# Turning the VectorE and ScalarE streams of a decode-attention kernel into hardware loops

## Chip, cores, metric

One core of one Trainium2 chip. The metric is device microseconds of one execution, as a median over runs; lower is better.

## The reference, cut to what matters

One token passes a block of attention over a long cache, beside a small feed-forward branch. With 32 heads of width 128 and 32768 cached positions in bf16, each head's K and each head's V are 8.39 MB. Together they are 537 MB of the 554 MB that the core reads.

```python
q = (xn @ wq).reshape(32, 128)                  # one token
scores = einsum("hd,hkd->hk", q, k) * 128**-0.5 # k: 32 x 32768 x 128
p = softmax(scores, -1)
o = einsum("hk,hkd->hd", p, v)
out = x + o.reshape(4096) @ wo + ffn(xn)
```

## The kernel before

SBUF holds a ring of three slots of 8.39 MB. SyncE streams wq, the feed-forward weights, K and V of every head and wo through it, and waits before each load until the slot's last reader has finished:

```python
for h in range(H):
    units.append(("k", h))
    if h >= 1: units.append(("v", h - 1))
units += [("wo",), ("v", H - 1)]
# SyncE, for each unit u in slot s
if s in owner: e.wait_ge(*owner.pop(s))
if u[0] == "k":
    e.dma_start(ring[:, s, :], kv_src(A_k_cache, u[1], 0, NJ)).then_inc(s_slot[s], 16)
    owner[s] = (s_qk, NHF * (u[1] + 1))     # free after TensorE has read the products
elif u[0] == "v":                           # the last V comes in five chunks (TAIL)
    e.dma_start(ring[:, s, :], kv_src(A_v_cache, u[1], 0, NJ)).then_inc(s_slot[s], 16)
    owner[s] = (s_pv, u[1] + 1)
```

For each head VectorE multiplies K by q in place, TensorE sums the products in part (against an identity), VectorE finishes the sums and the maximum, ScalarE takes the exponential, and TensorE multiplies by V one head later. TensorE's stream is already a hardware loop over groups of three heads. VectorE's and ScalarE's are written out for 32 heads:

```python
for h in range(H):                                    # VectorE
    v.wait_ge(s_qc, min(NQB, (h * DH) // 512 + 1))
    v.wait_ge(s_slot[s], 16 * use_of[u])              # K has landed
    q = qb[:, h * DH:(h + 1) * DH]
    for i in range(NHF):                              # 4 multiplies, 128 x 8192 bf16
        v.tensor_tensor(out=kh, in0=kh, in1=q[:, None, :].to_broadcast([128, HF, DH]),
                        op=ALU.mult).then_inc(s_mul, 1)
    ...                                               # 4 reduces, rz(h - 1)
    v.tensor_reduce(out=pmax[...], ...); v.wait_ge(s_t, h + 1)
    v.tensor_reduce(out=m1[...], ...);   v.wait_ge(s_b, h + 1)
    if h >= SR: v.wait_ge(s_exp, h - SR + 1)
    v.tensor_scalar(out=negb[...], ...).then_inc(s_neg, 1)

for h in range(H):                                    # ScalarE
    if h >= 3: column(h - 3)
    if h >= 2: evac(h - 2)
    a.wait_ge(s_neg, h + 1)
    ...                                               # two more waits
    a.activation(out=P[:, h % PR, :], in_=sc[:, :], func=ACTF.Exp, ...)
```

At the end TensorE has a long written-out tail: 155 products with wo for the first 31 heads, then 256 products with the last V, each a weight load and a product of one column:

```python
for h in range(H - 1): att(h)               # 5 products each
total(H - 1)
for i, n in enumerate(TAIL):                # pv_last: 256 products
    t.wait_ge(s_tail[i], 16)
    for _ in range(n):
        mm = t.matmul(OL, lhsT=ring[:, s, j*DH:(j+1)*DH], rhs=P[:, h % PR, j:j+1], ...)
        j += 1
```

## Time and profile before

| quantity | before |
|---|---|
| time, median of 3 runs | 1294.44 us (1294.24 to 1294.62) |
| bytes moved | 554.20 MB |
| share of DMA engines busy, middle of the run | 1.00 |
| VectorE idle before a head's first multiply | 2.8 us |
| instruction packets on queue 14 | 6 |

The first fence is the page of the profile. It gives each engine's busy time, the DMA totals, the queues (packets, MB, share of 16 engines' span), and the chain of work that ended last. PE is TensorE, PEld its weight loads, DVE VectorE, ACT ScalarE, POOL GpSimd, SPq SyncE's sequencer; L479 is line 479 of the kernel. The trace marks packets of the kind "instruction": six of 8192 bytes on queue 14 and nine on queue 8. They are taken for pieces of the engines' own programs, fetched while the program runs (in an experiment below, 1536 more VectorE instructions brought twelve more packets); below such a packet is called a refill.

```profile
span 1292.7 us, 9645 instructions
...
PE 1040.2 (80%) x5147; PEld 264.2 (20%) x3227; DVE 669.9 (52%) x407; ACT 50.8 (4%) x139; POOL 1.1 (0%) x8
...
DMA packets 14721, 554.20 MB, mean 429 GB/s; under 512 B 1329, under 2 KB 5490, under 8 KB 5746
...
q8 instruction: 9, 0.15, 0.0%
q14 instruction: 6, 0.05, 0.0%
...
DMA 54%; PE 30%; DVE 13%; issue 2%; SPq 1%; DVEq 0%
```

Next is the table by windows. Each row is a stretch of about three heads, with the busy time of the engines; the last three columns are the granted TensorE clock, the DMA share and GB/s.

```profile
core 0: us, PE busy (x) PEld busy (x) DVE busy (x) ACT busy (x) POOL busy (x), PEclk, DMA share, GB/s
366.60:482.80 116.20, 95.16 (x427) 22.43 (x246) 62.44 (x36) 4.11 (x12) 0.00 (x0) 0.90 1.00 433
715.00:831.00 116.00, 94.20 (x422) 22.03 (x241) 62.44 (x36) 4.10 (x12) 0.00 (x0) 0.90 1.00 433
```

In these stretches the DMA engines are busy all the time (share 1.00), at 433 GB/s. The chain of waits gives them only 54%, because it hops between loads and compute around the ring. The timeline of VectorE shows the slack (start, duration, what, then in brackets the idle time before and its releaser):

```profile
729.50 17.43 DVE L479 TENSOR_TENSOR ring<-ring,qb 128x8192 bf16<-128x8192 bf16 x4 [2.77 <-DMA ring<-in_A_k_cache_dram]
...
765.19 0.16 DVE L499 TENSOR_SCALAR negb<-ps 128x1 f32<-128x1 f32 x1 [6.94 <-PE ps L309]
769.18 4.43 DVE L479 TENSOR_TENSOR ring<-ring,qb 128x8192 bf16<-128x8192 bf16 x1 [3.83 <-DMA ring<-in_A_k_cache_dram]
```

VectorE is done with a head and then waits for the next K. The usual wait is 2.8 us. The last lines of the before kernel that matter are TensorE's in the tail:

```profile
1280.02 1.76 PE L279 MATMUL ps<-P,ring 128*128 128x1 bf16 x61
1282.06 3.55 PE L279 MATMUL ps<-P,ring 128*128 128x1 bf16 x128 [0.27 <-issue]
1285.80 1.50 PE L279 MATMUL ps<-P,ring 128*128 128x1 bf16 x51 [0.19 <-issue]
1287.88 0.59 PE L279 MATMUL ps<-P,ring 128*128 128x1 bf16 x16 [0.59 <-DMA ring<-in_A_v_cache_dram]
```

Its last 16 products wait for the last chunk of V: the end is bound by a landing.

### The profile page before, as it was taken

Reading aid. Unit: us, or ns where it says so; the run is one execution under the profiler, and the core shown is the slowest. Engines: PE = TensorE matmul, PEld = TensorE weight load, DVE = VectorE, ACT = ScalarE, POOL = GpSimd, SP = SyncE. Lnnn points to the kernel's source line nnn. Section 1 sums busy time; section 2 is a strip of 40 time slices with the busy share of each in tenths; the row PEclk is TensorE's granted clock in tenths of the full one; section 3 lists DMA queues with packets and bytes.
Section 4 is the critical chain, followed back from the end, with each engine's and each line's share of the span. In section 5 each row is a group of like instructions: output and inputs, shape, how many; then the busy total and the mean of one; then the engine's idle time right before and its main releaser. Section 6 shows DMA issues by size and latency. Waiting matters only on the chain.

```text
span 1292.7 us, 9645 instructions
## 1 busy us (share of the span) xinstructions
PE 1040.2 (80%) x5147; PEld 264.2 (20%) x3227; DVE 669.9 (52%) x407; ACT 50.8 (4%) x139; POOL 1.1 (0%) x8
## 2 busy tenths in 40 slices
PE   4688879877779877779877779877778877779878
PEld 1301222111222111222111222111222111222116
DVE  0485544666444666444666444666444666444660
ACT  2000000000000000000000000000000000000000
POOL 0000000000000000000000000000000000000000
PEclk9588899888899888889888889888899888899887
DMA  9999999999999999999999999999999999999997
GB/s 400 449 424 427 443 426 437 432 436 434 432 434 436 426 436 436 430 432 438 432 436 430 436 434 430 434 436 428 434 438 432 430 438 436 432 430 436 436 392 311
DMA packets 14721, 554.20 MB, mean 429 GB/s; under 512 B 1329, under 2 KB 5490, under 8 KB 5746
## 3 DMA queue, kind: packets, MB, share of 16 engines
q1 hardware_dynamic: 14704, 554.00, 99.4%
q8 instruction: 9, 0.15, 0.0%
q14 instruction: 6, 0.05, 0.0%
q10 hardware_dynamic: 2, 0.00, 0.0%
HBM read 553.99 MB, written 0.00 MB: 429 GB/s over the span
## 4 chain that ended last, share of the span: by engine, by line
DMA 54%; PE 30%; DVE 13%; issue 2%; SPq 1%; DVEq 0%
DMA ring<-in_A_k_cache_dram 52%; PE ps L266 16%; DVE ring L479 13%; PE ps L227 12%; DMA ring<-in_A_v_cache_dram 2%; PE ps L254 1%; SPq L174 1%; PE ps L303 0%; PE ps L297 0%; SPq L183 0%; DVE sc L485 0%; PE ps L279 0%; SPq L185 0%; DVE pmax L491 0%; SPq L182 0%
## 5 line engine op out<-in xcount | busy, mean ns | idle before, releaser
L479 DVE TENSOR_TENSOR ring<-ring,qb 128x8192 bf16<-128x8192 bf16 x128 | 557.8, 4421 | 88.4 <-DMA ring<-in_A_k_cache_dram 88.4
L227 PE MATMUL ps<-ring,ident 128*128 128x512 bf16 x1920 | 498.7, 418 | 0.0
L266 PE MATMUL ps<-ring,P 128*4 128x512 bf16 x1984 | 438.3, 379 | 0.0
L254 PE MATMUL ps<-ring,ident 128*128 128x512 bf16 x128 | 56.1, 439 | 224.2 <-DVE ring L479 223.6
L266 PEld LDWEIGHTS ps<-ring,P 128*4 128x4 bf16 x1984 | 166.0, 85 | 245.4
L254 PEld LDWEIGHTS ps<-ring,ident 128*128 128x128 bf16 x128 | 12.6, 99 | 622.2 <-DVE ring L479 350.4
L499 DVE TENSOR_SCALAR negb<-ps 128x1 f32<-128x1 f32 x32 | 5.1, 158 | 215.5 <-PE ps L309 215.5
L485 DVE TENSOR_REDUCE sc<-ps 128x64 f32<-128x512 f32 x128 | 82.3, 686 | 63.0 <-PE ps L227 63.0
L494 DVE TENSOR_REDUCE m<-ps 1x1 f32<-1x128 f32 x32 | 8.9, 278 | 192.2 <-PE ps L303 192.2
L403 ACT ACTIVATE P<-sc,negb 128x256 bf16<-128x256 f32 x32 | 16.2, 508 | 1185.1 <-DVE negb L499 1185.1
L297 PEld LDWEIGHTS ps<-rsum,ones 128*128 128x128 f32 x64 | 12.3, 194 | 99.1 <-issue 98.3
L289 PE MATMUL ps<-identf,o 4*128 4x1 f32 x248 | 31.8, 245 | 0.9 <-ACT o L386 0.9
L289 PEld LDWEIGHTS ps<-identf,o 4*128 4x128 f32 x248 | 30.0, 187 | 0.9 <-ACT o L386 0.9
L386 ACT ACTIVATE o<-ps,rzb 4x512 f32<-4x512 f32 x31 | 21.0, 677 | 0.0
L219 PE MATMUL ps<-ring 128*128 128x512 bf16 x40 | 11.3, 455 | 11.0 <-DMA ring<-in_A_wq_dram 11.0
L449 DVE TENSOR_SCALAR sg<-sg 128x13 f32<-128x13 f32 (+1 forms) x2 | 0.2, 156 | 34.2 <-ACT sg L379 34.2
L491 DVE TENSOR_REDUCE pmax<-sc 128x1 f32<-128x256 f32 x32 | 13.4, 420 | 0.0
L303 PE MATMUL ps<-identf,pmax 128*1 128x128 f32 x64 | 12.2, 273 | 1.2 <-DVE pmax L491 1.2
L330 PE MATMUL ps<-xn,ring 128*128 128x1 bf16 (+1 forms) x140 | 8.8, 199 | 4.6 <-DMA ring<-in_B_w_down_dram 4.6
L309 PE MATMUL ps<-m,ones 1*128 1x1 f32 x64 | 12.1, 256 | 0.4 <-DVE m L494 0.4
L309 PEld LDWEIGHTS ps<-m,ones 1*128 1x128 f32 x64 | 9.4, 182 | 14.2 <-issue 13.5
L468 DVE RECIPROCAL rzb<-ps 128x1 f32<-128x1 f32 x32 | 5.1, 158 | 9.8 <-PE ps L297 9.8
(50 smaller groups left out, 88.8 us busy)
## 6 DMA issues: line engine op xcount, KB each, us to landing
ring<-in_A_wq_dram SPq DMA_DIRECT2D x1, 5120.0 KB, 15.2
ring<-in_A_wo_dram SPq DMA_DIRECT2D x1, 5120.0 KB, 37.0
ring<-in_A_v_cache_dram SPq DMA_DIRECT2D x1, 4096.0 KB, 22.3
ring<-in_B_w_gate_dram SPq DMA_DIRECT2D x1, 2160.0 KB, 19.9
ring<-in_B_w_up_dram SPq DMA_DIRECT2D x1, 2160.0 KB, 24.6
ring<-in_B_w_down_dram SPq DMA_DIRECT2D x1, 2080.0 KB, 28.5
ring<-in_A_v_cache_dram SPq DMA_DIRECT2D x1, 2048.0 KB, 21.6
ring<-in_A_v_cache_dram SPq DMA_DIRECT2D x1, 1024.0 KB, 23.6
```

The lines of the kernel that those rows point to most:

```text
L174: e.dma_start(ring[:, s, j * DH:(j + n) * DH], kv_src(A_v_cache, u[1], j, n)).then_inc(s_tail[i], 16)
L227: return t.add_instruction(mybir.InstMatmult(start_tensor_calc=False, stop_tensor_calc=stop, tile_size=(128, 128), tile_position=(0, 0), l ...
L254: t.matmul(ob, lhsT=ident[:, :], rhs=src, start=True, stop=False)
L266: mm = t.matmul(O, lhsT=P[:, h % PR, j:j + W], rhs=ring[:, s, j * DH:(j + W) * DH], start=(j == 0), stop=(j + W == NJ))
L289: mm = t.matmul(fold_ps, lhsT=o4[:, m * DH:(m + 1) * DH], rhs=identf[0:W, m:m + 1], start=(m == 0), stop=(m == W - 1))
L297: t.matmul(misc[:, 129:130], lhsT=ones[:, :], rhs=rsum[:, h % SR:h % SR + 1], start=True, stop=True).then_inc(s_z, 1)
L309: t.matmul(misc[:, 128:129], lhsT=ones[0:1, :], rhs=m1[0:1, h % SR:h % SR + 1], start=True, stop=True).then_inc(s_b, 1)
L386: a.activation(out=o4[:, :], in_=O, func=ACTF.Copy, scale=rzb[0:W, h % SR:h % SR + 1]).then_inc(s_o4, 1)
L403: a.activation(out=P[:, h % PR, :], in_=sc[:, :], func=ACTF.Exp, bias=negb[:, h % SR:h % SR + 1], scale=c_scale, accum_out=rsum[:, h % SR: ...
L479: v.tensor_tensor(out=kh, in0=kh, in1=q[:, None, :].to_broadcast([128, HF, DH]), op=ALU.mult).then_inc(s_mul, 1)
L485: v.tensor_reduce(out=sc[:, i * HF:(i + 1) * HF], in_=bank[i].rearrange("p (j e) -> p j e", e=G), axis=AX.X, op=ALU.add).then_inc(s_red, 1)
L491: v.tensor_reduce(out=pmax[:, h % SR:h % SR + 1], in_=sc[:, :], axis=AX.X, op=ALU.max).then_inc(s_max, 1)
```

## The change

The intent is to give the two engines short programs: their streams become hardware loops of three heads a turn. Wait counts become register values (`group * d + n`), and the q and ocol addresses become register offsets. To make all counts positive and linear, ScalarE raises `s_ov` once at the start and its readers wait for one more. Waits that others imply are dropped. VectorE's loop starts at head 2, ScalarE's at head 5. The diff, cut:

```diff
+        def counter(e, h0):
+            group = [None]
+            def wait(sem_of, h, count):
+                n = count(h)
+                if group[0] is not None:
+                    d = count(h + PER) - n
+                    ...
+                    n = group[0] * d + n
+                e.wait_ge(sem_of, n)
+            return group, wait
+        def at(tile, h, n, i):
+            start = h * n if i is None else i * (PER * n) + h * n
+            return tile[:, bass.ds(start, n)]
 ...  ScalarE
+                a.sem_inc(s_ov, 1)
-                for h in range(H):
-                    ...
-                    if h >= PR: a.wait_ge(s_pv, h - PR + 1)
-                    if h >= SR: a.wait_ge(s_z, h - SR + 1)
+                for h in range(HA):
+                    step(h)
+                with a.Fori(0, (H - HA) // PER) as i:
+                    group[0] = i
+                    for h in range(HA, HA + PER):
+                        step(h)
 ...  VectorE
-                    if h >= SR: v.wait_ge(s_o4, h - SR + 1)
-                    q = qb[:, h * DH:(h + 1) * DH]
+                    q = at(qb, h, DH, group[0])
-                    v.wait_ge(s_qk, h * NHF + i + 1)
+                    wait(s_qk, h, lambda h: h * NHF + i + 1)
-                    if h >= SR: v.wait_ge(s_exp, h - SR + 1)
 ...
+                with v.Fori(0, (H - H0) // PER) as i:
+                    group[0] = i
+                    for h in range(H0, H0 + PER):
+                        head(h)
```

## The prediction

1294.0 us is the 1294.44 us measured before, less about 0.4 us.

> **What bounds it now.** The DMA engines. In the table by windows, nine stretches of three heads (116 us each, 134 to 1180 us) show a DMA share of 1.00 to 1.01 and 432 to 435 GB/s; only the last 12 us fall to 0.39. The DMA table has 554.2 MB in 14721 packets: at the steady 433.5 GB/s that is about 1278 us of the 1292.7 us span. [...] A head takes 38.7 us (K-load issues at 571.4, 610.15, 648.8 us in the timeline), about what its 16.8 MB need.
>
> The chain of waits names K loads for only 52%, as it hops between loads and compute around a ring of three slots. The timeline shows the slack: VectorE is idle 2.8 us before each head's first multiply, waiting for K; and a K load lands 41.9 us after issue (V 36.8) though its bytes take 19.4 us at 433 GB/s. So 17 to 22 us of earlier loads are still queued when one is issued. Compute must be over 2.8 us per head slower on average, or over some 17 us late once, before the DMA runs dry.
>
> **What the change does.**
> - Multiplies, reduces and activations stay. The multiply (4.42 us for 128x8192 bf16, 128 times) takes q at an address from a register. [...] I expect 4.42 us again.
> - Added on VectorE: about ten register waits a head, one to two register instructions each, a q address, and one branch per three heads. TensorE's loop in this trace prices them: register instructions 32 to 37 ns, following each other at about 100 ns; compare-and-branch 208 ns. Estimate: 1 to 2 us of sequencer time a head, nearly all behind running multiplies or inside waits (6.9 us before negb, 6.2 us before m, 2.8 us before the multiply). Exposed on the compute chain: perhaps 0.1 to 0.5 us a head, below 2.8.
> - Added on ScalarE: the same, smaller; it is 4% busy. Removed: a few implied waits, 21 to 38 ns each.
> - Removed: most refills of instructions for these two engines: six packets of 8 KB in the run (four VectorE, two ScalarE by spacing), 0.32 us each on one of 16 DMA engines. Spread over 16 engines that is 0.1 us; if one lagging engine carries all, 1 to 2 us. TensorE's refills stay.
> - Start and tail: unchanged; VectorE leaves its loop well before the last V chunk lands.
>
> **On the critical path:** nearly nothing.
>
> **Prediction: 1294.0 us, range 1291.5 to 1297.0.** Faster by over 2%: 1%; within 2%: 97%; slower by over 2%: 2%.
>
> **Right if** the windows still show share 1.00 at 433 GB/s and 116 us per three heads; VectorE's wait for K falls from 2.8 us a head by at most 0.5 us and stays positive; instruction packets of queue 14 fall from 6 to 1 to 3; VectorE has hundreds of register instructions.
>
> **Wrong if** [...] a loop body does not stay resident and each of ten turns waits for a refill behind saturated queues, which shows only over some 8 us a turn; or if register waits stall VectorE by several us a head. Then the DMA share drops below 1.00.

## The result, and the profile after

| | before | after |
|---|---|---|
| first measurement, 4 runs each | 1294.53 us (1294.24 to 1294.67) | 1293.75 us (1293.55 to 1293.82) |
| second measurement, 9 and 5 runs | 1294.07 us (1293.93 to 1294.50) | 1293.60 us (1293.52 to 1293.78) |
| ratio, 95% interval | | 0.9993 [0.9979, 1.0007]; 0.9996 [0.9982, 1.0010] |

A ratio is the mean time of one kernel's runs over that of the other's of the same rounds, so it is not quite the ratio of the medians quoted. The change is worth nothing that counts. Still, in neither measurement does a run of after reach the fastest run of before; the gap of 0.5 to 0.8 us is below what the intervals resolve, but the traces say where it comes from.

The page after shows nearly the same totals, except that queue 14 carries two instruction packets instead of six:

```profile
span 1292.1 us, 9830 instructions
...
PE 1036.7 (80%) x5147; PEld 263.8 (20%) x3227; DVE 669.9 (52%) x407; ACT 51.9 (4%) x139; POOL 1.1 (0%) x8
...
DMA packets 14717, 554.16 MB, mean 429 GB/s; under 512 B 1329, under 2 KB 5490, under 8 KB 5746
...
q8 instruction: 9, 0.15, 0.0%
q14 instruction: 2, 0.02, 0.0%
...
DMA 52%; PE 29%; DVE 12%; issue 6%; SPq 0%; DVEq 0%; ACT 0%
```

The windows are the same:

```profile
core 0: us, PE busy (x) PEld busy (x) DVE busy (x) ACT busy (x) POOL busy (x), PEclk, DMA share, GB/s
366.60:482.80 116.20, 95.22 (x428) 22.51 (x247) 62.43 (x36) 4.23 (x12) 0.00 (x0) 0.90 1.00 433
715.00:831.00 116.00, 94.83 (x427) 22.40 (x246) 62.44 (x36) 4.23 (x12) 0.00 (x0) 0.90 1.00 432
```

The added register work shows in the view of one source line. "DVEq" is VectorE's sequencer; the numbers are count, then minimum, median and maximum duration in ns. L162 is the helper for waits, L529 the loop itself:

```profile
L162 DVEq ALU_OP  x150: 40/40/52, 122.4 to 1254.4; - x150
L162 DVEq FUSED_REGOPS  x20: 46/53/53, 111.8 to 1155.5; - x20
```

```profile
L529 DVEq FUSED_REGOPS  x10: 63/63/63, 111.4 to 1152.5; - x10
L529 DVEq COMPARE_BRANCH  x10: 50/56/67, 223.4 to 1268.3; - x10
```

With the 30 that form q's address and 10 for the loop counter, that is 220 register instructions and 10 branches: 0.36 us a looped head from the recorded durations ((160 x 40 + 60 x 62 + 10 x 57 ns) / 30). Nearly all of them sit behind running work. VectorE's timeline for the same two heads differs in one place:

```profile
729.39 17.43 DVE L504 TENSOR_TENSOR ring<-ring,qb 128x8192 bf16<-128x8192 bf16 x4 [2.77 <-DMA ring<-in_A_k_cache_dram]
...
765.10 0.16 DVE L522 TENSOR_SCALAR negb<-ps 128x1 f32<-128x1 f32 x1 [6.93 <-PE ps L322]
768.09 4.43 DVE L504 TENSOR_TENSOR ring<-ring,qb 128x8192 bf16<-128x8192 bf16 x1 [2.84 <-DMA ring<-in_A_k_cache_dram]
```

VectorE finishes head 18 at the same time in both, but K of head 19 lands 1 us earlier after the change. Comparing the start of every head's first multiply, the kernel after is level with before (within 0.2 us) up to head 10, and then draws ahead in three steps: by 0.24 us at head 11, 0.99 us at head 19, 0.98 us at head 27. Head 31 starts at 1232.50 us instead of 1234.59 us.

Each step falls in the interval in which before has a small packet on queue 14, at 445.0, 755.5 and 1066.2 us; an earlier one is at 127.1 us. At 445.0, 755.5 and 1066.2 us VectorE had issued 193, 321 and 449 recorded instructions, 128 more each time (from the packet at 127.1 us to the one at 445.0 us it is 132), and each packet has 8192 bytes. So these are taken to be VectorE's own refills, 128 instructions each; the experiments below test it. Two more, at 383.5 and 1199.4 us, are 126 recorded ScalarE instructions apart. They leave no step.

The DMA records show what a refill does. K and V packets run back to back on each engine, so packets can be sorted into 16 chains, each starting where the one before ended (this assignment to engines is inferred, as the records name none). From the DMA records of before, by this chaining:

```
start us   took us  bytes   (chain with VectorE's refills)
753.132    2.418    65536
755.546    0.324     8192   instruction refill
755.858    3.081    65536   usual: 2.42

start us   took us  bytes   (chain with ScalarE's refills)
381.042    2.418    65536
383.456    0.314     8192   instruction refill
383.767    2.801    65536
```

VectorE's refill cost the engine that carried it 0.32 us plus 0.66 us on the packet after it: 0.98 us. All four VectorE refills lie on one chain, ScalarE's two on another (0.69 us each). TensorE's, of 16384 bytes, cost 1.57 us at 139.1 and at 178.0 us (1.02 + 2.97 - 2.42) and 1.09 us at 218.9 us (1.08 + 2.43 - 2.42), on three different chains.

The author's reading of this: a load has landed when its slowest engine is done, so lags on one DMA engine add up, and of different engines the largest counts. It is tested below (twelve more VectorE refills: 11.77 us; a lag on ScalarE's engine beside VectorE's: 4.90 us, not their sum of 7.6 us). By this reading, before, VectorE's engine lags 4 x 0.98 = 3.92 us; after, one refill is left on it (0.98 us), and an engine with a TensorE refill of 1.57 us is the slowest. The difference is 2.35 us; measured at head 31: 2.09 us, or 2.24 us counted from head 10, where the kernel after is 0.16 us behind.

Then most of it is given back. In TensorE's tail, after:

```profile
1277.93 1.76 PE L292 MATMUL ps<-P,ring 128*128 128x1 bf16 x61
1279.93 3.55 PE L292 MATMUL ps<-P,ring 128*128 128x1 bf16 x128 [0.23 <-issue]
1285.86 1.92 PE L292 MATMUL ps<-P,ring 128*128 128x1 bf16 x67 [2.38 <-issue]
1288.10 0.36 PE L358 MATMUL ps<-ocol,ring 128*128 128x1 bf16 x5 [0.32 <-DVE ocol L538]
```

TensorE no longer waits for the last chunk of V. It now stands still for 2.38 us after product 189 of 256, with no data missing. The gaps are exactly 128 products (256 instructions) apart, one refill of 16384 bytes. TensorE's products end at 1287.78 us instead of 1288.47 us: 0.69 us are left of 2.09.

The packets say what this stop waits for. In all twelve kept traces with a stop at a block boundary in the tail (all but that of the 5 us delay below), TensorE resumes 1.3 to 1.5 us after a refill's packet has landed: before, at 1285.80 after 1284.52 us; after, at 1285.86 after 1284.60 us. So this refill came at nearly the same time in both kernels, and in the kernel after TensorE only reached the boundary earlier. By the chaining, in both kernels the packet starts when its DMA engine has just written its last piece of V (1283.46 and 1283.53 us). In the kernel before that is 4.4 us ahead of the last landing, so this is not the engine that VectorE's refills had held up, and removing them did not bring it forward.

### The profile page after: what moved, and what is told of

The parts are those of the page before. It is cut to its first block, busy times and chain, and to the rows that moved or that the text cites. A ratio compares the mean times of both kernels' runs of the same rounds, so it can differ in the third digit from the quotient of the medians.

```text
span 1292.1 us, 9830 instructions
## 1 busy us (share of the span) xinstructions
PE 1036.7 (80%) x5147; PEld 263.8 (20%) x3227; DVE 669.9 (52%) x407; ACT 51.9 (4%) x139; POOL 1.1 (0%) x8
## 4 chain that ended last, share of the span: by engine, by line
DMA 52%; PE 29%; DVE 12%; issue 6%; SPq 0%; DVEq 0%; ACT 0%
DMA ring<-in_A_k_cache_dram 52%; PE ps L279 17%; DVE ring L504 12%; PE ps L248 9%; PE ps L267 1%; PE ps L292 1%; PE ps L358 1%; PE ps L316 0%; PE ps L310 0%; PE ps L302 0%; DVEq L504 0%; SPq L204 0%; DVE sc L510 0%; PE ps L322 0%; ACT o L403 0%
## 5 line engine op out<-in xcount | busy, mean ns | idle before, releaser
L504 DVE TENSOR_TENSOR ring<-ring,qb 128x8192 bf16<-128x8192 bf16 x128 | 557.8, 4420 | 86.6 <-DMA ring<-in_A_k_cache_dram 86.5
```

## The experiments

**Only the loops undone; then one loop at a time.** Is it the loops or the edits to the waits, and which engine's loop? The three edits to the kernel after:

```diff
 # e3_unrolled: both of these; e1_vector_only: the first; e2_scalar_only: the second
-                for h in range(HA):
-                    step(h)
-                with a.Fori(0, (H - HA) // PER) as i: ...
+                for h in range(H):
+                    step(h)
-                with v.Fori(0, (H - H0) // PER) as i: ...
+                for h in range(H0, H):
+                    head(h)
```

> The kernel after with both loops written out again (all its edits to waits kept, only the two hardware loops undone). Theory (each 8 KB instruction refill of VectorE takes 0.98 us from always the same one of the 16 DMA engines, and that engine sets the landing of every load): VectorE again issues some 480 instructions, so again 3 to 4 refills in the run, the first multiply of head 31 again at about 1234 us and the time again 1294.3 to 1294.7 us. Rival (the edits to the waits, not the loops, made the 0.8 us): time 1293.6 to 1293.9 us and head 31 at about 1232.3 us.

> Only VectorE's loop; ScalarE written out. Theory (ScalarE's two refills go through another DMA engine, which stays ahead of the slowest): head 31's first multiply at 1232.3 us as in the kernel after, queue 14 with two more instruction packets than after (about 4), time 1293.5 to 1294.0 us. Rival (each refill costs wherever it goes): head 31 later than 1232.3 us by 0.7 to 1.4 us.

> Only ScalarE's loop; VectorE written out. Theory: as the kernel before: VectorE's refills at four places, head 31's first multiply at 1234.0 to 1234.4 us, time 1294.3 to 1294.7 us. Rival (ScalarE's loop brings its share): head 31 earlier than 1234 us by 0.7 us or more.

Against before at 1294.27 us (9 runs, 1294.12 to 1295.07): both loops undone 1294.41 us, only VectorE's loop 1294.01 us (1293.41 to 1294.13), only ScalarE's loop 1294.43 us. The times hardly tell them apart; the timelines do. Head 31's first multiply with both undone, with only VectorE's loop, and with only ScalarE's:

```profile
1234.77 17.43 DVE L499 TENSOR_TENSOR ring<-ring,qb 128x8192 bf16<-128x8192 bf16 x4 [2.84 <-DMA ring<-in_A_k_cache_dram]
```

```profile
1232.62 17.43 DVE L499 TENSOR_TENSOR ring<-ring,qb 128x8192 bf16<-128x8192 bf16 x4 [2.85 <-DMA ring<-in_A_k_cache_dram]
```

```profile
1234.70 17.43 DVE L504 TENSOR_TENSOR ring<-ring,qb 128x8192 bf16<-128x8192 bf16 x4 [2.74 <-DMA ring<-in_A_k_cache_dram]
```

The 2 us come with VectorE's loop alone. With ScalarE written out, its one refill (422 us) costs nothing that head 31 shows (1232.62 us, 1232.50 us in the kernel after). The count of packets there was expected to be 4 and was 2, as ScalarE issues fewer instructions once the waits are gone. With VectorE written out but with fewer waits, its refills move to 127, 474, 823 and 1172 us, and the steps move with them: only ScalarE's loop is 0.9 us ahead of before at head 19 and level again at head 31. With only VectorE's loop the time was 1294.01 us (after, in other rounds: 1293.75 us); its earlier landing is given back in the tail too, with a stop of 1.0 us.

**More refills of VectorE.** First a failed try, with empty instructions in the kernel before:

```diff
+                    for _ in range(64):
+                        v.nop(nofuse=True)
                     v.wait_ge(s_b, h + 1)
```

> The kernel before with 64 empty instructions a head on VectorE, in its 6.9 us wait ahead of negb, so that VectorE fetches some 19 or 20 blocks instead of 4. Theory (0.98 us of one DMA engine per block, adding up): about 15 or 16 more refills, 14 to 16 us longer, 1308 to 1311 us, all of it as later landing of loads; VectorE keeps waiting about 2.8 us a head for K or longer. Rival (a refill costs its bytes, 0.02 us over 16 engines, and the 1 us steps are something else): 1294.5 us. Second rival (the empty instructions themselves delay VectorE): negb later and VectorE's wait for K shrinks.

Measured 1294.23 us, with 9645 instructions and six packets, as before: the compiler had dropped them. It says nothing of the theory, and serves as a repeat of before. The second try used real work:

```diff
+        spare = sbt("spare", [128, 48], F32)
+                    for x in range(48):
+                        v.memset(spare[0:1, x:x + 1], 0.0)
                     v.wait_ge(s_b, h + 1)
```

> In the run before, the compiler dropped the empty instructions, so that it was the kernel before once more. This time 48 real one-element memsets a head on VectorE in the kernel before, in its 6.9 us wait ahead of negb. Theory (each block of 128 VectorE instructions is one 8 KB refill that takes 0.98 us from one and the same DMA engine, and these add up): about 16 refills instead of 4, first multiply of head 31 about 11.8 us later (1246 us), time 1304 to 1308 us. Rival (a refill costs its bytes alone): no change, 1294.3 us. Second rival (the memsets delay VectorE itself): negb comes later after TensorE's product than 0.16 us and VectorE's wait for K shrinks below 2.8 us.

Measured 1306.24 us (1305.41 to 1307.09) against 1294.61 us. The queue's line and then VectorE's timeline from head 16 to 17 and at head 31:

```profile
q14 instruction: 18, 0.15, 0.0%
```

```profile
693.74 0.16 DVE L502 TENSOR_SCALAR negb<-ps 128x1 f32<-128x1 f32 x1 [5.87 <-PE ps L310]
697.71 4.43 DVE L480 TENSOR_TENSOR ring<-ring,qb 128x8192 bf16<-128x8192 bf16 x1 [3.81 <-DMA ring<-in_A_k_cache_dram]
...
1246.36 8.76 DVE L480 TENSOR_TENSOR ring<-ring,qb 128x8192 bf16<-128x8192 bf16 x2 [3.82 <-DMA ring<-in_A_k_cache_dram]
```

Twelve more packets, and head 31 starts 11.77 us later: 0.98 us each, as the packet records said. VectorE still waits for K, longer than before where a refill fell in between, and negb is still released by TensorE. So it is the landing that is late, not VectorE.

**The same instructions inside the loop.** The memsets added to the kernel after:

```diff
+                    for x in range(48):
+                        v.memset(spare[0:1, x:x + 1], 0.0)
                     wait(s_b, h, lambda h: h + 1)
```

> The same 48 memsets a head in the kernel after: as many instructions executed, but in a loop body of some 250 instructions (three heads). Theory A (the body of two to three blocks of 128 stays resident): queue 14 as in the kernel after, up to two packets more, 1293.5 to 1294.5 us. Theory B[...]: two to three refills at every one of ten turns, 20 to 30 more packets, 1313 to 1323 us.

Measured 1293.50 us (1293.29 to 1294.17) against 1294.61 us, with four packets:

```profile
q14 instruction: 4, 0.03, 0.0%
```

The trace counts 203 VectorE instructions a turn (the estimate had been 250; the body after has 59). Three packets come before 214 us, the last two of them in the loop's first turn, and none at any later turn; the fourth comes after the loop, at 1274 us, as one does in the kernel after (1272.6 us). Head 31 starts at 1233.84 us, 1.34 us later than in the kernel after. The lags say the same: three refills on VectorE's DMA engine are 2.94 us, where after TensorE's 1.57 us was the largest. The time does not show these 1.34 us, as the tail takes them up (stops of 0.46 and 0.74 us). So 1536 more executed instructions cost no more than the two refills that came with them, while the 12 refills of the run above cost 11.6 us: the cost is in fetching, not in executing.

**More refills of ScalarE.** Do lags on two engines add?

```diff
+                    for x in range(48):
+                        a.activation(out=spare[0:1, 48 * (h % 3) + x:48 * (h % 3) + x + 1],
+                                     in_=xq[0:1, 0:1], func=ACTF.Copy)
                     a.wait_ge(s_neg, h + 1)          # kernel before
```

> 48 one-element activations a head on ScalarE in the kernel before, in its 37 us wait ahead of the exponential: some 14 refills of ScalarE instead of 2, which pass through another DMA engine than VectorE's and take 0.69 us each there. Theory (the slowest of 16 DMA engines sets every landing: the lags of two engines do not add, the larger counts): ScalarE's engine lags 14 x 0.69 = 9.3 to 9.7 us, VectorE's 4 x 0.98 = 3.9 us, so head 31 starts about 5.4 to 5.8 us later than before, time 1299 to 1301 us. Rival (lags add): 8.3 us later, 1302 to 1303.5 us. Rival (no cost): 1294.3 us.

Measured 1299.52 us (1299.43 to 1300.06) against 1294.61 us, and 18 packets. Head 31:

```profile
1239.49 13.10 DVE L482 TENSOR_TENSOR ring<-ring,qb 128x8192 bf16<-128x8192 bf16 x3 [2.85 <-DMA ring<-in_A_k_cache_dram]
```

That is 4.90 us later than before. ScalarE had 13 refills by then, one of them at 47 us in the start-up: 12 or 13 times 0.69 us minus VectorE's 3.92 us is 4.4 to 5.1 us. (The forecast of 5.4 to 5.8 us had counted 14.) Adding the lags would have given about 7.6 us, 0.69 us for each of the 11 more refills. The larger lag counts.

**How much slack compute has.** A delay on VectorE between K's landing and the first multiply of each looped head, in the kernel after:

```diff
+                    if group[0] is not None:
+                        v.tensor_reduce(out=spare[:, 0:1], in_=qb[:, 0:1920], axis=AX.X, op=ALU.max)
                     for i in range(NHF):             # 5 us: two reduces of 0:2400
```

> The kernel after with one added reduce of 1920 bf16 elements (estimated 2.0 us[...]) between K's landing and the first multiply in each of the 30 looped heads. Theory of the prediction (compute has 2.8 us of slack a head against the loads): no change in time, 1293.4 to 1294.6 us; VectorE's idle time before K falls from 2.8 to about 0.8 us a head, DMA share stays 1.00. Rival (loads and compute alternate, as the chain of waits with its 52% DMA looks): 30 x 2 = 60 us longer, 1354 us.

> The same with two reduces of 2400 elements (estimated 5.1 us a head). Theory: 5.1 minus 2.8 is 2.3 us a head beyond the slack, 30 heads: about 65 to 72 us longer, 1356 to 1366 us, VectorE no longer waits for K and the DMA share falls to about 0.94. Rival (alternating): 30 x 5.1 = 153 us longer, 1447 us. If the reduces take another time than estimated, the excess over 2.8 us times 30 holds.

The added 2.0 and 5.1 us were estimates. VectorE's reduces of before (128x512 in 686 ns, 128x256 in 420 ns: 1.04 ns a column) would give 2.0 and 5.0 us. In the runs one reduce of 1920 took 2.15 us, one of 2400 took 2.65 us.

With 2 us: 1293.92 us (before: 1294.07 us). VectorE's waits, in total, count and longest us, for the shorter delay:

```profile
DVE spare L504 <- DMA ring<-in_A_k_cache_dram: 20.5, 27, 0.8
```

VectorE took 62 us more work and only its wait shrank, from 2.8 to 0.8 us a head. With 5 us: 1365.51 us (1365.36 to 1365.96), ratio 1.0552 [1.0536, 1.0568]. Its windows:

```profile
core 0: us, PE busy (x) PEld busy (x) DVE busy (x) ACT busy (x) POOL busy (x), PEclk, DMA share, GB/s
599.00:715.00 116.00, 87.79 (x394) 19.52 (x213) 77.36 (x41) 4.23 (x12) 0.00 (x0) 0.87 0.96 407
```

The two reduces moved the first multiply by 5.13 us (604.45 to 609.58 us in the timeline). 5.13 minus 2.8 us, times 30 heads, is 70 us; measured 71.4 us against before, 71.9 us against after. Loads and compute run side by side, and the 54% of the chain of waits is no measure of what the DMA costs.

**The stop in the tail.** 156 more instructions early in TensorE's stream shift all later ones in their blocks:

```diff
+                for _ in range(78):
+                    t.matmul(ps8[0:1, 5, 300:301], lhsT=one1[:, :], rhs=one1[:, :],
+                             start=True, stop=True)
                 t.wait_ge(s_a, 11)
```

> The kernel after with 78 dummy one-element matrix products (156 instructions) early on TensorE, in its 11 us wait for wq: the same work, but every later TensorE instruction lies 156 places further on in its blocks of 256. Theory (in the kernel after, the last V chunks land 2 us earlier, but TensorE stands still 2.4 us at a block boundary in its last products, waiting for its own refill): the boundary moves from 67 products before the end to about 17 before the end, where TensorE waits for the last V chunk anyway; time 1291.5 to 1293.0 us. Rival (the tail is bound by the work or by the landing, not by refills): 1293.5 to 1294.0 us as the kernel after.

Measured 1294.68 us (1293.84 to 1295.11) against 1294.61 us. The hoped-for gain did not come: the time is that of before, outside both ranges, though head 31 started 1.90 us earlier than in before. TensorE's timeline:

```profile
1277.68 0.68 PE L360 MATMUL ps<-ocol,ring 128*128 128x1 bf16 x14 [0.41 <-issue]
...
1278.65 3.10 PE L294 MATMUL ps<-P,ring 128*128 128x1 bf16 x111
1283.81 3.55 PE L294 MATMUL ps<-P,ring 128*128 128x1 bf16 x128 [2.06 <-issue]
1287.83 0.59 PE L294 MATMUL ps<-P,ring 128*128 128x1 bf16 x17 [0.46 <-issue]
```

The boundary moved just as computed, to products 111 and 239 of 256, and a stop of 2.06 us went with it. So the stop belongs to the block boundary and not to a chunk's landing. But this shift did not remove it: TensorE runs through a block in 3.55 us, and the refills before the stop landed 6.2 us apart here and 6.1 us apart in the kernel after. A stop is not there in every run: in the run delayed by 5 us the refills landed at 1351.17 and 1355.70 us, and TensorE went through all 256 products in 6.96 us.

**After once more.**

> The kernel after once more beside before, to see whether the first small difference repeats. Theory (2.1 us of DMA time gained, most of it given back in TensorE's last 6 us): 0.3 to 1.0 us below before, first multiply of head 31 at 1232.2 to 1232.5 us, and at least 1.5 us in which TensorE stands at a block boundary in the last V products.

Measured 1293.60 us against 1294.07 us, stops of 0.45 and 1.83 us in the tail, and head 31 2.04 us earlier than in the first trace of before. It repeats.

No version here is clearly faster than after. The looped memsets measured 1293.50 us, but their runs (1293.29 to 1294.17 us) span those of after.

## Why the prediction was right or wrong

- **DMA-bound, with 2.8 us of compute slack a head: right.** The windows kept 1.00 and 433 GB/s, and a delay of 2 us a head vanished while one of 5.13 us cost 71 us.
- **The multiply keeps its time of 4.42 us: right.** 4420 ns with a register address, 4421 ns before. Why it would, no run here shows.
- **Added register work hidden: right; its size is not settled.** There were 7.3 register instructions a head, not ten waits with one or two each. Their recorded durations are 0.36 us a head. The forecast of 1 to 2 us was of sequencer time, which is not the same: in the trace of after, VectorE's register instructions in a row mostly start 222 to 240 ns apart, and 267 ns after a branch. On the compute chain, a register instruction of 64 ns follows K's landing where a 21 ns wait stood.
- **Refills fall from six to 1 to 3: right (two). Their worth: the term was mis-sized.** The prediction counted 0.32 us a refill. The packet behind it takes another 0.66 us, so it is 0.98 us, and all four of VectorE's fall on one engine. The branch "if one lagging engine carries all, 1 to 2 us" was the nearer one, at 2.09 us; "spread over 16 engines 0.1 us" was not. But its sum was another: six refills of 0.32 us, where the record has VectorE's four of 0.98 us less the 1.57 us of a TensorE refill that stays.
- **"Start and tail: unchanged": right for the start, wrong for the tail.** The tail turned from waiting for the last V chunk to waiting at TensorE's block boundaries, and gave 1.4 us back. So the time moved by 0.5 to 0.8 us, close to the 0.4 us predicted, but that closeness is luck: two misses, 2.1 us gained and 1.4 us given back, nearly cancel.
- **Loop body not resident: did not happen**, nor with 203 instructions a turn.

What stays open: why the refill at 1283.5 us started only when, by the chaining, its DMA engine had no V left to write (in the run with 156 more instructions one went between two V packets, at 1281.42 us); how much of the 2.09 us would have come through without the stop, which no run removed from the kernel after alone; and why a refill slows the next packet by 0.66 us on one engine and 0.38 us on another.

## What to carry to other kernels

When the DMA engines are full (share 1.00 here), look at what rides on a single one of them: here the largest lag on any one engine set when the loads landed, and 8 KB of instructions cost 0.98 us where their bytes are worth 0.02 (8192 bytes at 433 GB/s). Turning a written-out stream into a loop was here worth its refills and no more, and the register work was free because VectorE waits 2.8 us a head for data anyway. Before counting on an earlier landing, ask what else the last engine waits for; here it was its own instructions.
